# Attention beside a long convolution on one core: the convolution's weights without zeros, two lags per matmul

## The chip, the cores and the metric

The kernel runs on one core of a Trainium2 chip. The core has a matmul engine (TensorE, PE in the profile, with PEld for its weight loads), a vector engine (VectorE, DVE), an engine for activation functions (ScalarE, ACT), a general one (GpSimd, POOL) and SyncE (SP), which here only issues DMAs. The metric is the time of one execution on the device in microseconds (us), less is better.

## The reference

Two independent halves are computed from bf16 inputs of 2048 positions, and their outputs stand side by side in the last dimension (512 + 512 columns).

The first half is softmax attention with 32 heads of 16 channels:

```
qkv = x @ wqkv                          # 2048 x 512 @ 512 x 1536
p   = softmax(q k^T / 4)                # 32 heads, 2048 x 2048 each
a   = (p v) @ wo
```

The second half is a convolution over the whole sequence, one filter of 2048 taps for each of 512 channels:

```
k_shift[t] = sum over m < 4 of k[t-m] * shift_k[:, m]
kv = k_shift * v
y[t] = sum over s <= t of ssm_k[:, t-s] * kv[s]      # written with FFTs in the reference
b  = q * (y + kv * ssm_D)
```

## The kernel before, in words

**Attention.** The scores are made transposed, in blocks of 128 keys x 512 queries for one head. There are 32 x 16 x 4 = 2048 such blocks. `qk_mm` (line 796) makes three or so at once, as a head has only 16 channels (padded to 32 rows) and four row strips of PE can hold four heads. A block fills one of the eight PSUM banks. Banks 0 to 2 and 3 to 5 take turns for ScalarE, bank 6 collects the weighted sums, and bank 7 (`BGB`) serves everything else: projections, the convolution, the output projection, and extra score blocks for VectorE.

`emit_exp` (line 821) has ScalarE take the exponential of two or three banks in one instruction, and writes it to the ring PT. `exp_on_dve` (lines 884 to 905) does it on VectorE for some blocks: one instruction takes a block out of PSUM, five more for two blocks at a time make three terms whose sum is the exponential. `emit_pv` (line 970) multiplies by the values; a block of ScalarE needs one matmul, a block of VectorE three.

In `emit_qk` (lines 734 to 740) a block for VectorE goes to bank 7 if that is free (`dve_block(T, n)`). If it is not, and VectorE has little left to do (`LOW`), the block takes the third of the banks that ScalarE would have used, and ScalarE's instruction covers two banks only.

**The convolution.** A Toeplitz product on PE. `kz_store` reverses the filters, adds `ssm_D` to the tap of lag 0 and stores them to a DRAM scratch tensor. `feed_wr` (line 1152) loads a filter back into a row of the ring WR with a source step of one element per partition, so that partition i holds the filter shifted by i. KV holds the products of key and value; they are the weights of the matmul (`lhsT`), and the filter is what is streamed (`rhs`, 128 columns). In the kernel before, the two halves of the 128 partitions hold neighbouring blocks of 64 positions, interleaved by partition (`KV[ch:128:2]`), and where the other block is missing the weights are zeros. `conv_lags` (line 1187) makes 32 lags for each of 64 steps of 8 channels. Each lag is four matmuls, one per column strip of 32: 64 x 32 x 4 = 8192. `conv_out` copies the result out of bank 7 (line 1207), `conv_turn` turns it round on PE (line 1219) and VectorE multiplies by q (line 1226). KV is filled by a product on VectorE (line 561) into a staging area and spread by four DMAs for each 128 channels (`spread_kv`).

**The order of the work.** The program is straight-line code, with the order made in Python when the kernel is built. A planner keeps a clock per engine, with fixed costs for each kind of instruction, and goes in steps T, one ScalarE instruction of line 821 each. In each step it places the next scores, then the weighted sums of step T - 2, then background work that fits before the next exponential: projection halves and other jobs with due times (`jobs`, `unit_step`), and convolution lags, at most `LAGS` a step, from step `N_OPEN` on and spread by `conv_due` up to step `PLAN`. What is left of PE's time gets filler matmuls on zeros (`warm_up`, line 1382). `release` lets SP issue filter loads at chosen points of PE's order. Semaphores hold each engine to that order; every engine runs its own list strictly in turn.

All DMAs are issued through line 352, on three queues: SP (inputs, filters, KV), POOL (spreading of the queries QT, the convolution's q and output, the attention output) and ScalarE (two first weights and the last store).

Of the kernel before, what the change touches and what calls it, by code (L numbers as in the profile page):

```python
# [13 lines left out]
S = 2048  # L14
# [13 lines left out]
NLAG = S // 64  # L28
PAD = 128
LKZ = PAD + S  # L30
LEFT = 16
LKR = LEFT + S
R_W = 12
R_PT = 16
# [8 lines left out]
LEAD = 2  # L43
YIELD = -4
FIRST = 6
BURST = 2
OVER_C = 0.0
HURRY = 2
LOW = 4.5
# [20 lines left out]
R_PTD = 3  # L70
# [12 lines left out]
PLAN = 588  # L83
# [4 lines left out]
GAP = 5  # L88
# [7 lines left out]
DMA_KB = 394  # L96
X_KB = 200
# [24 lines left out]
WR_KB = 330  # L122
# [132 lines left out]
def bass_concat_heads__mha_block__ssm_conv_h3__prompt_kernel(  # L255
# [13 lines left out]
    kz_ap = nc.dram_tensor("kz_scratch", (C, LKZ), BF16).ap()  # L269
# [10 lines left out]
    def sb(name, shape, dt=BF16):  # L280
# [13 lines left out]
    QN = QNF[:, 0:NB * 256].rearrange("p (t d) -> p t d", t=NB)  # L294
# [13 lines left out]
    PTD = sb("PTD", [128, R_PTD, 3, 2, QB])  # L308
    FR = sb("FR", [128, 2 * QB])
# [7 lines left out]
           for x in (WR[:, R_W - 2, :], WR[:, R_W - 1, :], OUTA[:, :, :].rearrange("p r d -> p (r d)"), VS2[:, :])]  # L317
# [9 lines left out]
    KVF = KV[:, :, :, :, :].rearrange("p o r u g -> p (o r u g)")  # L327
    STG = [KVF[:, 32 * S // 16 * ((c + 1) % 4):32 * S // 16 * ((c + 1) % 4 + 1)].rearrange(
        "p (h o u k g) -> p h o u k g", h=2, o=16, u=NB, k=2) for c in range(4)]
    XN = FR[:, :].rearrange("p (j f) -> p j f", j=2)  # L330
# [66 lines left out]
    d_wr = [DmaSem(sem(f"d_wr{i}")) for i in range(3)]  # L397
# [25 lines left out]
    for c in range(4):  # L423
        src = bass.AP(tensor=v2.tensor, offset=v2[128 * (NB - 1), 128 * c].offset, ap=[[D, 128], [-128 * D, NB], [1, 128]])
        h_vn.append(dma(sp, d_kv[3 + c], VST[c], src, kb=512))
# [18 lines left out]
    h_kv0 = [None, None]  # L444
    h_kv0[0] = pool.op(lambda e: e.memset(KV[:, :, :, :, :].rearrange("p o r u g -> p (o r u g)").bitcast(U32), 0), us=(8.8, 8.9))
# [25 lines left out]
    def ready(u):  # L471
# [8 lines left out]
        return KT_OF[u[1]][0] in h_kt and (u[1] < 3 or h_kv0[1] is not None and at(h_kv0[1]) <= pe.t)  # L480

    def pe_unit(u, bank, parts=(0, 1, 2, 3)):
# [19 lines left out]
        elif kind == "kv":  # L502
# [31 lines left out]
    def evac_unit(u, bank, h):  # L534
# [18 lines left out]
        elif kind == "kv":  # L553
            _, c, i = u
            u0 = NB - 4 - 4 * i
            val = VST[c][:, u0:u0 + 4, :].rearrange("p b (h o g) -> p b h o g", h=2, g=4)
            src = PS[:, bank, :].rearrange("p (b h o g) -> p b h o g", b=4, h=2, g=4)
            for ch in range(2):
                dst = STG[c][:, ch, :, u0:u0 + 4, ch, :].rearrange("p o u g -> p u o g")
                hh = (dve.op if ch else urgent)(  # L560
                    lambda e, dst=dst, ch=ch: e.tensor_tensor(dst, src[:, :, ch], val[:, :, ch], ALU.mult),
                    [h, h_vn[c], h_kv0[c // 3]], us=(0.335, 0.46))
# [3 lines left out]
            if sum(kv_n[0:2]) == 8 and c < 2:  # L566
                load_qn(0, [h])
                open_wr(2, hh, True)
# [13 lines left out]
    def spread_kv(c, hh):  # L582
        for half in range(2):
            for ch in range(2):
                src = STG[c][64 * half:64 * half + 64, ch].rearrange("p o u k g -> p o (u k g)")
                dst = KV[ch:128:2, 16 * c:16 * c + 16, 1 - half, :, :].rearrange("p o u g -> p o (u g)")
                h_kvc[c] = dma(sp, d_kvc[c], dst, src, [hh, h_kvc[c - 1] if c else None] if half + ch == 0 else [], kb=256, rate=210)
# [930 lines left out]
```

## Time and profile before

| | us |
|---|---|
| median of 3 runs | 810.54 (809.68 to 813.88) |
| the profiled execution | 807.64 |
| its span | 805.7 |
| ScalarE busy | 784.9 (97%) |
| PE busy | 745.7 (93%) |
| VectorE busy | 715.1 (89%) |
| POOL busy | 90.4 (11%) |

The granted TensorE clock was 0.999 over the execution. The DMA queues moved 161.44 MB, 150.43 MB of it on SP's queue, which took 58.2% of the time of the 16 DMA engines.

A group's row reads: line, engine, operation, output <- inputs, shapes, count | busy us, mean ns of one | idle time of the engine just before, and what ended it. The mean time of one instruction includes its latency; instructions of one engine overlap at their ends, so counts times means come to more than the busy time. A row with "(+1 forms)" mixes shapes. In a row of waits stand the total, the number and the longest. A row of the timeline begins with its start and its length in us.

### The profile page before, as it was taken

How to read it: one execution, taken by the hardware profiler on the slowest of the kernel's cores; microseconds unless marked ns; L12 is line 12 of the kernel's file. 1: busy time of each engine (PE TensorE's matmuls, PEld its weight loads, DVE VectorE, ACT ScalarE, POOL GpSimd, SP SyncE). 2: the span in 40 equal slices, each digit the busy share in tenths (PEclk: the TensorE clock that was granted, in tenths of full speed). 3: DMA queues.
4: the chain of work that ended last, by engine and by line, in shares of the span. 5: the costliest groups of instructions: out<-in, count | busy, mean ns of one | idle time of the engine just before them, and what ended most of it. 6: DMA issues, size and time to landing. Idle time of an engine off the chain costs nothing.

```text
span 805.7 us, 31982 instructions
## 1 busy us (share of the span) xinstructions
PE 745.7 (93%) x14505; PEld 337.1 (42%) x14505; DVE 715.1 (89%) x1427; ACT 784.9 (97%) x680; POOL 90.4 (11%) x160
## 2 busy tenths in 40 slices
PE   8889998999998989999999989989989899999987
PEld 3333444435444433444433434434443434434444
DVE  5989999999798989898898989889999899889986
ACT  7999999999999999999999999999999999999997
POOL 6200402020100101020010030101003020000000
PEclk9999999999999999999999999999999999999999
DMA  9995277846877671446845657985684663876310
GB/s 244 204 306 175 63 184 227 287 108 215 265 261 240 215 243 59 156 115 235 267 142 206 213 168 254 308 281 193 227 299 138 212 224 129 283 260 216 110 55 28
DMA packets 88101, 161.44 MB, mean 200 GB/s; under 512 B 49216, under 2 KB 53184, under 8 KB 87584
## 3 DMA queue, kind: packets, MB, share of 16 engines
q1 hardware_dynamic: 80976, 150.43, 58.2%
q0 software_dynamic: 5792, 8.66, 3.7%
q8 instruction: 114, 1.87, 0.9%
q10 hardware_dynamic: 1200, 0.33, 0.2%
q14 instruction: 19, 0.16, 0.1%
HBM read 142.87 MB, written 6.42 MB: 185 GB/s over the span
## 4 chain that ended last, share of the span: by engine, by line
ACT 79%; PE 14%; DVE 5%; issue 1%; DMA 1%
ACT PT L821 79%; PE PS L970 5%; PE PS L796 4%; PE PS L1187 1%; DVE PTD L884 1%; DMA QN<-in_B_k_dram 1%; PE PS L512 1%; PE PS L1115 1%; PE PS L630 0%; PE PS L491 0%; DVE PTD L902 0%; DVE DT L1041 0%; DVE PTD L905 0%; DVE FR L892 0%; DVE PTD L896 0%
## 5 line engine op out<-in xcount | busy, mean ns | idle before, releaser
L821 ACT ACTIVATE PT<-PS 128x1024 bf16<-128x1024 f32 (+1 forms) x674 | 781.9, 1362 | 11.5 <-PE PS L796 10.8
L796 PE MATMUL PS<-QT,KTo 32*128 32x512 bf16 (+2 forms) x2248 | 265.6, 364 | 39.8 <-ACT PT L821 17.5
L884 DVE TENSOR_SCALAR PTD<-PS 128x512 uint16<-128x512 f32 x326 | 219.2, 682 | 49.2 <-PE PS L796 47.8
L1187 PE MATMUL PS<-WR,KV 128*26 128x128 bf16 (+9 forms) x8192 | 191.2, 219 | 0.7 <-issue 0.6
L970 PE MATMUL PS<-PT,VA 128*32 128x512 bf16 (+2 forms) x1889 | 184.6, 369 | 5.0 <-DVE DT L1041 2.1
L1187 PEld LDWEIGHTS PS<-WR,KV 128*32 128x32 bf16 (+8 forms) x8192 | 140.6, 94 | 52.9 <-issue 29.8
L796 PEld LDWEIGHTS PS<-QT,KTo 32*128 32x128 bf16 x2248 | 69.6, 91 | 205.0 <-ACT PT L821 150.4
L970 PE MATMUL PS<-PTD,VA 128*32 128x512 bf16 (+1 forms) x1077 | 121.0, 360 | 3.9 <-issue 3.9
L902 DVE TENSOR_TENSOR PTD<-FR,PTD 128x1024 f16<-128x1024 bf16 (+1 forms) x164 | 112.3, 685 | 4.0
L905 DVE TENSOR_TENSOR PTD<-PTD 128x1024 bf16<-128x1024 f16 (+1 forms) x164 | 111.5, 680 | 1.9
L352 POOL DMA_DIRECT2D QT<-QS x120 | 60.4, 511 | 443.7 <-DVE QS L539 443.7
L970 PEld LDWEIGHTS PS<-PT,VA 128*32 128x32 bf16 x1889 | 47.4, 93 | 100.8 <-issue 85.5
L892 DVE TENSOR_SCALAR FR<-PTD 128x1024 uint16<-128x1024 uint16 (+1 forms) x164 | 69.0, 421 | 3.5
L896 DVE TENSOR_SCALAR PTD<-PTD 128x1024 uint16<-128x1024 uint16 (+1 forms) x164 | 68.9, 420 | 0.0
L1382 PE MATMUL PS<-IDN,ZW 128*32 128x512 bf16 (+3 forms) x297 | 67.4, 310 | 1.3 <-issue 1.0
L899 DVE TENSOR_SCALAR PTD<-FR 128x1024 f16<-128x1024 bf16 (+1 forms) x164 | 68.1, 415 | 0.0
L970 PEld LDWEIGHTS PS<-PTD,VA 128*32 128x32 bf16 x1077 | 44.8, 96 | 33.2 <-issue 4.4
L1382 PEld LDWEIGHTS PS<-IDN,ZW 128*32 128x32 bf16 x297 | 23.4, 96 | 23.3 <-issue 12.2
L1041 DVE STREAM_TRANSPOSE DT<-PS 128x512 f32<-128x512 f32 x31 | 22.1, 713 | 5.6 <-PE PS L970 5.3
L352 POOL DMA_DIRECT2D out_dram<-OUTA x15 | 8.6, 575 | 97.2 <-DVE OUTA L1123 93.1
L1115 PE MATMUL PS<-WKV,OTN 128*128 128x512 bf16 (+1 forms) x68 | 19.0, 371 | 0.3 <-DVE OTN L1090 0.3
L523 PE MATMUL PS<-WKV,xT 128*128 128x128 bf16 x256 | 18.3, 220 | 0.4 <-DVE KTo L548 0.3
(75 smaller groups left out, 259.3 us busy)
## 6 DMA issues: line engine op xcount, KB each, us to landing
WR<-kz_scratch SPq DMA_DIRECT2D x256, 512.0 KB, 5.8
KV<-KV SPq DMA_DIRECT2D x16, 256.0 KB, 5.4
kz_scratch<-WR SPq DMA_DIRECT2D x1, 2176.0 KB, 8.8
QN<-in_B_q_dram POOLq DMA_DIRECT2D x2, 1024.0 KB, 7.6
out_dram<-QN POOLq DMA_DIRECT2D x2, 1024.0 KB, 8.3
QT<-QS POOLq DMA_DIRECT2D x120, 16.0 KB, 3.3
out_dram<-OUTA POOLq DMA_DIRECT2D x15, 128.0 KB, 2.0
QN<-in_B_ssm_k_dram SPq DMA_DIRECT2D x1, 1024.0 KB, 8.3
```

The lines of the kernel that those rows point to most:

```text
L352: f(outp, inp).then_inc(dsem.sem, 16)
L796: ins = e.matmul(PS[:, bank, i * w:i * w + w], lhsT=KTo[32 * s:32 * s + 32, OF[n_] % 2, kt * 128:(kt + 1) * 128], rhs=QT[32 * s:32 * s + 3 ...
L821: h_exp[T] = act.op(lambda e: e.activation(PT[:, p0:p0 + n, :].rearrange("p b f -> p (b f)"), PS[:, banks[0]:banks[0] + n, :].rearrange("p ...
L884: st["h"].append(urgent(lambda e: e.tensor_scalar(lin[:, QB * half:QB * half + QB].bitcast(U16), PS[:, bank, :], FIX_ADD, FIX_HI, ALU.add, ...
L892: st["d"] = st["m"] = dve.op(lambda e: e.tensor_scalar(FR[:, w].bitcast(U16), lin[:, w].bitcast(U16), 0x7F, 0x3F80, ALU.bitwise_and, ALU.b ...
L896: dve.op(lambda e: e.tensor_scalar(low[:, w].bitcast(U16), lin[:, w].bitcast(U16), 0xFF80, None, ALU.bitwise_and), [st["h"][-1]], us=us)
L899: st["d"] = dve.op(lambda e: e.tensor_scalar(top[:, w].bitcast(FP16), FR[:, w], T1, T0, ALU.mult, ALU.add), [st["m"]], us=us)
L902: st["d"] = h_last[j] = dve.op(lambda e: e.tensor_tensor(top[:, w].bitcast(FP16), FR[:, w], top[:, w].bitcast(FP16), ALU.mult), [st["d"]], ...
L905: st["d"] = dve.op(lambda e: e.tensor_tensor(top[:, w], top[:, w].bitcast(FP16), lin[:, w], ALU.mult), [st["d"]], us=us)
L970: ins = e.matmul(dst, lhsT=w, rhs=rhs, start=first, stop=last, tile_position=(0, 32 * s))
L1187: ins = e.matmul(PS[32 * g:32 * g + 2 * ((30 - d) // 2 + 1), BGB, c0:c0 + w], lhsT=kv, rhs=WR[:, (4 * qd + g) % R_W, S - 64 * d - 128:S - ...
L1382: pe.op(lambda e, s=s, k=k, rhs=rhs, bank=bank, rows=rows, c0=c0, first=first: e.matmul(PS[32 * s:32 * s + rows, bank, c0:c0 + 128 * k], l ...
```

## The change

The convolution's partitions are laid out anew. Partitions 0 to 63 take positions of the first half of the sequence (0 to 1023) and partitions 64 to 127 those of the second, in blocks of 64. For each lag block the stationary operand holds both halves of the partitions filled with data, and the streamed filter row holds the filter at two offsets that lie 1024 taps apart. One matmul so does what two did, no weights are zeros between, and there are 8 lags for each of 128 steps of 4 channels (`NLAG`, `NQD`): 128 x 8 x 4 = 4096 matmuls, each of 128 streamed columns, with 32, 30, ... 18 columns of weights in place of 32, 32, 30, ... 2.

The filters are stored in DRAM by channel pairs: for each pair and each half of the partitions, 2 x 1088 taps one after the other (`SEG` = 1088). One DMA loads 64 partitions with runs of 2112 elements (4224 bytes), two channels at once; there are 512 such loads in place of 256 of 128 partitions with runs of 4096 bytes. The ring WR has room for 22 of them (11 rows of both halves).

Along with it:

- KV is half as large. Products of key and value go straight to it, in one instruction of 512 columns in place of two of 256, and the second copy for the other half of the partitions is made by one DMA per 128 channels in place of four. The matmuls before it write 64 rows each, two at once. Its second clearing in the middle of the kernel falls away.
- The convolution is done in bursts of four steps (`BURST`) that fill bank 7, and copied out 512 columns at a time; turning the result round takes eight matmuls for 8 steps (16 x 8 = 128) where four transposes for 4 steps (16 x 4 = 64) stood.
- q and the convolution's output are loaded and stored as halves of 64 partitions, four DMAs each in place of two; v is loaded in halves too.
- On VectorE's path for exponentials the three terms get two rings: five buffers for the first term (`PTD`), three for the other two (`RST`), with the steps in another order. `next_blocks` and `dve_block` choose blocks by row strip.
- A block for VectorE is no longer held back from bank 7 when the convolution wants it but has no room in this step (`state["go"]`, `PRESS`).
- Constants of the planner change, R_PT from 16 to 15 among them, and due times of some jobs are spread.

Counted in the lists of the two programs as built (before / after): exponentials of three banks 374 / 463, of two banks 300 / 162; score blocks taken by VectorE 326 / 335; its five-step chains 164 / 169; fillers 297 with 101,504 columns / 564 with 207,360; matmuls in all 14,505 / 11,014.

```diff
-NLAG = S // 64
+NLAG = S // 256
+NQD = C // 4
+SEG = S // 2 + 64
-R_W = 12
-R_PT = 16
+R_W = 22
+R_PT = 15
-BURST = 2
+BURST = 4
-LOW = 4.5
+LOW = 3.0
-PLAN = 588
+PLAN = 600
-WR_KB = 330
+WR_KB = 300
...
-    kz_ap = nc.dram_tensor("kz_scratch", (C, LKZ), BF16).ap()
+    kz_ap = nc.dram_tensor("kz_scratch", (C // 2, 2, 2 * SEG), BF16).ap()
...
-    WR = sb("WR", [128, R_W, S])
+    WR = sb("WR", [128, R_W // 2, SEG + S // 2])
-    KV = sb("KV", [128, C // 8, 2, 2 * NB, 4])
+    KV = sb("KV", [128, NQD, 2 * NB, 4])
...
                 for m in range(4):
-                    c0 = LEFT + 128 * (4 * i + 3 - b) - m
-                    ins = e.matmul(PS[:, bank, 128 * b:128 * b + 128], lhsT=KTR[kt_i][:, kt_c, c0:c0 + 128], rhs=DG[:, c, m, :],
-                                   start=(m == 0), stop=(m == 3))
+                    for x in range(2):
+                        c0 = LEFT + 64 * (4 * i + 3 - b) + S // 2 * x - m
+                        ins = e.matmul(PS[64 * x:64 * x + 64, bank, 128 * b:128 * b + 128], lhsT=KTR[kt_i][:, kt_c, c0:c0 + 64],
+                                       rhs=DG[:, c, m, :], start=(m == 0), stop=(m == 3), tile_position=(0, 64 * x))
...
+            dst = KV[:, 32 * c:32 * c + 32, u0:u0 + 4, :].rearrange("p q w g -> p w q g")
+            hh = urgent(lambda e: e.tensor_tensor(dst, src, val, ALU.mult), [h, h_vn[c]], us=V512)
...
+        src = KV[0:64, 32 * c:32 * c + 32, 0:NB, :].rearrange("p q w g -> p q (w g)")
+        dst = KV[64:128, 32 * c:32 * c + 32, NB:2 * NB, :].rearrange("p q w g -> p q (w g)")
+        h_kvc[c] = dma(sp, d_kvc[c], dst, src, [hh, h_kv0, h_kvc[c - 1] if c else None], kb=256, rate=KV_KB)
...
-        h_kzw[0] = dma(sp, d_kzw, kz_ap.rearrange("(p c) m -> p c m", c=4), KZS, [h, h_kz0], kb=2176)
+        for i in range(4):
+            r, x = i // 2, i % 2
+            dst = kz_ap.rearrange("(p r) x (c m) -> p r x c m", r=2, c=2)[:, r, x, :, :]
+            h_kzw[0] = dma(sp, d_kzw, dst, KZS[:, 2 * r:2 * r + 2, S // 2 * x:S // 2 * x + SEG], [h, h_kz0] if i == 0 else (), kb=557)
...
-        if aside and conv_wants(T):
+        if aside and conv_wants(T) and (state["go"] or conv_due() < T - PRESS):
             return None
...
-        lin, low, top = [PTD[:, j % R_PTD, i, :, :].rearrange("p a n -> p (a n)") for i in range(3)]
+        lin = PTD[:, j % R_PTD, :, :].rearrange("p a n -> p (a n)")
+        low, top = [RST[:, j % R_RST, i, :, :].rearrange("p a n -> p (a n)") for i in range(2)]
...
+            qd, r, x = n // 4, n % 4 // 2, n % 2
+            src = kz_ap[channel(qd) // 2 + r, x, 0:1]
+            src = bass.AP(tensor=kz_ap.tensor, offset=src.offset, ap=[[1, 64], [1, SEG + S // 2]])
+            h_wr[qd] = dma(sp, d_wr[qd % 6], WR[64 * x:64 * x + 64, (2 * qd + r) % (R_W // 2), :], src, [h_kzw[0], dep, h], kb=264, rate=WR_KB, late=2.95)
...
+    def conv_place(qd, g, rows):
+        dst = PS[32 * g:32 * g + rows, BGB, :]
+        c0 = 256 * (1 - qd % 4 // 2) + 64 * (1 - qd % 2)
+        return bass.AP(tensor=dst.tensor, offset=PS[32 * g:32 * g + 1, BGB, c0:c0 + 1].offset, ap=[dst.ap[0], [128, 2], [1, 64]])
...
-                d = DIST[n]
-                w = 64 if d < 0 else 128
                 for g in range(4):
-                    kv = KV[:, qd, (1 + d) % 2, (1 + d) // 2 * 2:2 * NB, g]
-                    ins = e.matmul(PS[32 * g:32 * g + 2 * ((30 - d) // 2 + 1), BGB, c0:c0 + w],
-                                   lhsT=kv, rhs=WR[:, (4 * qd + g) % R_W, S - 64 * d - 128:S - 64 * d - 128 + w],
+                    dst = conv_place(qd, g, 32 - 2 * n)
+                    w0 = SEG * (g % 2) + S // 2 - 128 * n - 128
+                    ins = e.matmul(dst, lhsT=KV[:, channel(qd) // 4, 2 * n:2 * NB, g], rhs=WR[:, (2 * qd + g // 2) % (R_W // 2), w0:w0 + 128],
                                    start=(n == 0), stop=(n == NLAG - 1), tile_position=(0, 32 * g))
...
+        src = bass.AP(tensor=src.tensor, offset=PS[:, BGB, 511:512].offset, ap=[src.ap[0], [-1, 512]])
+        bank_free[BGB] = h_ybw[0] = urgent(lambda e: e.tensor_copy(YB[:, qd % 8 // 4, :], src), [h, h_yb[0]], slack=S_C, us=V512)
...
             for k in range(4):
-                ins = e.transpose(pbf[:, 128 * k:128 * k + 128], YB[:, b % 2, 128 * k:128 * k + 128], IDN[:, :])
+                for part in range(2):
+                    y = YB[:, k // 2, 256 * (k % 2) + 128 * part:256 * (k % 2) + 128 * part + 128]
+                    ins = e.matmul(PS[:, bank, 128 * k + 4 * part:128 * k + 128], lhsT=y, rhs=(own, next_)[part], start=part == 0, stop=part == 1)
```

More of the change, by code (lines that the diff above doesn't have):

```diff
@@ L869, in dve_block @@
             return None
-        rows = [blk(b)[2] for b in bl[:-1]]
-        ahead = [b for b in ahead[:4] if b not in bl]
-        return next((b for b in ahead if blk(b)[2] not in rows), ahead[0] if ahead else None)
+        return pick_row(ahead, 4)
     h_last = {}
@@ L908, in exp_on_dve @@
         dep = lambda: [st["d"]]
-        begin = lambda: (n == 2 or st["alone"]) and (j == 0 or j - 1 in h_last)
+        begin = lambda: (n == 2 or st["alone"]) and (j < R_RST or all((j - R_RST, i) in h_ptd for i in range(len(pairs[j - R_RST]["h"]))))
         if half == 0:
@@ L949, in emit_pv @@
             pv_n[(n, s)] = pv_n.get((n, s), 0) + 1
-            terms = [PTD[:, on_dve[b][0] % R_PTD, i, on_dve[b][1], :] for i in range(3)] if b in on_dve else [PT[:, pt_of[b], :]]
+            terms = [PT[:, pt_of[b], :]] if b not in on_dve else [PTD[:, on_dve[b][0] % R_PTD, on_dve[b][1], :]] + [
+                RST[:, on_dve[b][0] % R_RST, i, on_dve[b][1], :] for i in range(2)]
             hl = 2 * s + n % 2
@@ L991, in conv_done @@
     def conv_done():
-        return state["qd"] == C // 8 and not state["turn"] and not part[0]
+        return state["qd"] == NQD and not state["turn"] and not part[0]
     def pv_step(T):
@@ L1213, in conv_turn @@
     def conv_turn(b, bank):
-        pbf = PS[:, bank, :].bitcast(BF16)
+        own, next_ = [bass.AP(tensor=IDN[:, :].tensor, offset=IDN[0:1, 31:32].offset, ap=[IDN[:, :].ap[0], [-1, n], [32, 4]]) for n in (32, 31)]
         def fn(e):
```

179 lines of the change are left out of this document (88 added, 91 removed).

## The prediction

> **What bounds the kernel now.** I read the shares of the engines first, then the chain that ended last, then the exponentials by shape, then what ScalarE and VectorE wait for.
>
> ```profile
> span 805.7 us, 31982 instructions
> ...
> PE 745.7 (93%) x14505; PEld 337.1 (42%) x14505; DVE 715.1 (89%) x1427; ACT 784.9 (97%) x680; POOL 90.4 (11%) x160
> ...
> ACT 79%; PE 14%; DVE 5%; issue 1%; DMA 1%
> ...
> L821 ACT ACTIVATE PT<-PS 128x1024 bf16<-128x1024 f32 (+1 forms) x674 | 781.9, 1362 | 11.5 <-PE PS L796 10.8
> ```
>
> ScalarE is busy for 97% of the span and carries 79% of the chain, and nearly all its work is one line, the exponential of line 821: 781.9 us, with 10.8 us of waits for the score matmuls of line 796. PE at 93% is a pipelined figure; it matters only where it makes ScalarE wait. So the change is worth what it takes off line 821's total and off those waits, and costs what it adds to them.
>
> The exponentials come in two shapes, by the groups kept apart by form, and at the very end the timeline of ScalarE shows the short one alone and in a row:
>
> ```profile
> L821 ACT ACTIVATE PT<-PS 128x1536 bf16<-128x1536 f32 x374 | 524.9, 1558 | 2.8 <-PE PS L796 2.5
> L821 ACT ACTIVATE PT<-PS 128x1024 bf16<-128x1024 f32 x300 | 301.1, 1117 | 8.7 <-PE PS L796 8.3
> ...
> 796.35 1.02 ACT L821 ACTIVATE PT<-PS 128x1024 bf16<-128x1024 f32 x1 [0.25 <-PE PS L796]
> 797.83 2.88 ACT L821 ACTIVATE PT<-PS 128x1024 bf16<-128x1024 f32 x3 [0.46 <-PE PS L796]
> ```
>
> One short exponential takes 1.02 us alone and three take 2.88, so each further one costs (2.88 - 1.02) / 2 = 0.93 us. The long ones then cost (781.9 - 300 x 0.93) / 374 = 1.345 us. Per block of 512 columns this is 0.465 us in the short form and 0.448 in the long one. The short form also meets most of the waits (8.3 of 10.8 us).
>
> **The change on ScalarE.** Lines 737 to 740 make a short exponential where a block for VectorE has to take one of ScalarE's three banks because bank 7 is occupied, mostly by a convolution. With half the convolution matmuls that bank is free more often. In the instruction list of the changed program, as built, there are 463 long and 162 short exponentials: 1713 blocks in place of 1722, in 625 instructions in place of 674. At the two prices: 463 x 1.345 + 162 x 0.93 = 773.4 us, which is 8.5 us less. One end: if time went by blocks alone, 9 x 0.465 = 4.2 us. The other: the mean times of the two rows, scaled so that they add up to 781.9 (524.9 + 301.1 = 826.0 counts overlaps), are 1.329 and 0.950 us; they give 769.2 us, 12.7 less. I take 8.5, since it rests on intervals and not on latencies.
>
> **The change on PE.** The next rows are the stretch of the convolution, from its first to its last matmul (length, busy time of PE, of its weight loads, VectorE, ScalarE, POOL, then clock, share of the DMA engines, GB/s), a run of convolution matmuls in the timeline, three groups, and three rows of PE's own waits (us in total, times, the longest).
>
> ```profile
> 106.00:767.00 661.00, 617.21 (x12846) 279.78 (x12838) 592.31 (x1169) 652.84 (x565) 59.85 (x112) 1.00 0.63 210
> ...
> 507.45 0.73 PE L1187 MATMUL PS<-WR,KV 128*32 128x128 bf16 x40
> ...
> L1187 PE MATMUL PS<-WR,KV 128*26 128x128 bf16 (+9 forms) x8192 | 191.2, 219 | 0.7 <-issue 0.6
> L523 PE MATMUL PS<-WKV,xT 128*128 128x128 bf16 x256 | 18.3, 220 | 0.4 <-DVE KTo L548 0.3
> L1382 PE MATMUL PS<-IDN,ZW 128*32 128x512 bf16 (+3 forms) x297 | 67.4, 310 | 1.3 <-issue 1.0
> ...
> PE PS L970 <- issue: 5.2, 7, 1.3
> PE PS L796 <- DVE PTD L884: 2.7, 8, 0.6
> PE PS L970 <- DVE DT L1041: 2.1, 6, 0.5
> ```
>
> The run is ten groups of four matmuls (four column strips), the first ten of a step, with 32 to 24 columns of weights; it takes 0.73 us, of which one matmul's own 0.22 is the drain: (0.73 - 0.22) / 9 = 0.057 us per group. The new form has 8 lags x 128 steps = 1024 groups in place of 2048, of the same 128 columns, so PE gets back 1024 x 0.057 = 58 us, or at 0.73 / 10 = 0.073 each, 75 us, at most. Against it: turning the result round becomes 128 matmuls in place of 64, at 18.3 / 256 = 0.071 us each 4.6 us; the key-value product has 512 in place of 256, which costs 0 if two column halves run side by side, as four strips do above, or 256 x 0.071 = 18 us if not. I take 0, because the strips are the nearer row. The fillers of line 1382 rise from 297 (101,504 columns) to 564 (207,360), by 67.4 x 207,360 / 101,504 - 67.4 = 70 us of busy time, but they are put only where PE would wait. So PE's share will hardly fall, and the 58 us shorten nothing by themselves. What they can shorten is the 10.8 us: the share of the waits that stands behind convolution bursts and short exponentials. Ends: all 10.8 gone, or 5 us more, if PE's own waits for issue and for VectorE (5.2 + 2.7 + 2.1 = 10 us in the rows above) grow by half and all of it reaches ScalarE. I take 3 us, a bit over a quarter, as the short form, which has 8.3 of them, falls by nearly half while code fetches and projections keep theirs.
>
> [...]
>
> **The change on VectorE.**
>
> ```profile
> L884 DVE TENSOR_SCALAR PTD<-PS 128x512 uint16<-128x512 f32 x326 | 219.2, 682 | 49.2 <-PE PS L796 47.8
> L902 DVE TENSOR_TENSOR PTD<-FR,PTD 128x1024 f16<-128x1024 bf16 (+1 forms) x164 | 112.3, 685 | 4.0
> L905 DVE TENSOR_TENSOR PTD<-PTD 128x1024 bf16<-128x1024 f16 (+1 forms) x164 | 111.5, 680 | 1.9
> L892 DVE TENSOR_SCALAR FR<-PTD 128x1024 uint16<-128x1024 uint16 (+1 forms) x164 | 69.0, 421 | 3.5
> L896 DVE TENSOR_SCALAR PTD<-PTD 128x1024 uint16<-128x1024 uint16 (+1 forms) x164 | 68.9, 420 | 0.0
> L899 DVE TENSOR_SCALAR PTD<-FR 128x1024 f16<-128x1024 bf16 (+1 forms) x164 | 68.1, 415 | 0.0
> ...
> L1207 DVE CAST YB<-PS 128x256 bf16<-128x256 f32 x32 | 13.3, 416 | 5.8 <-PE PS L1187 3.0 <-PE PS L970 2.3 <-PE PS L1382 0.4
> L1123 DVE CAST OUTA<-PS 128x512 bf16<-128x512 f32 x15 | 10.2, 682 | 0.4 <-PE PS L1115 0.4
> ```
>
> Nine more blocks: 9 x 219.2 / 326 = 6.1 us. Five more runs of the five-step chain (169 in place of 164): 5 x (112.3 + 111.5 + 69.0 + 68.9 + 68.1) / 164 = 13.1 us. The copy out of the convolution's bank is 512 wide in place of 256: 32 x (0.682 - 0.416) = 8.5 us. The 32 half products of key and value become 16 whole ones, about even. The sum is 28 us: 743 us busy of 794, 94%. VectorE's idle time falls from 91 to 51 us; 47.8 of the 91 were waits for score matmuls, which hide the additions, so on the path I count nothing. If that cover is gone, the rows above in which PE waits for VectorE (2.7 and 2.1 us) grow first.
>
> **The change on the queues.**
>
> ```profile
> WR<-kz_scratch SPq DMA_DIRECT2D x256, 512.0 KB, 5.8
> ...
> L352 SPq DMA_DIRECT2D WR<-kz_scratch x256: 512/606/1702, 50.5 to 751.0; - x128
> ...
> q1 hardware_dynamic: 2129, 7.74, 55.0%
> ...
> q1 hardware_dynamic: 4160, 1.05, 79.0%
> ...
> q1 hardware_dynamic: 5070, 1.34, 109.7%
> ```
>
> The filter loads become 512 of 64 partitions x 4224 bytes in place of 256 of 128 x 4096: 138.4 MB for 134.2. SP issues 256 more at 0.606 us, 155 us more on a queue that mostly waits. The last three rows are 40 us with filter loads alone on the queue (400 to 440 us), 6.5 us of a copy KV to KV whose source is 64 partitions (350 to 356.5), and 6 us of loads of v into all 128 partitions (22 to 28). The filter loads run at 7.74 / (0.55 x 40) = 352 GB/s of engine time. The copy and the loads of v, both in runs of 256 bytes, make 1.05 / (0.79 x 6.5) = 204 and 1.34 / (1.097 x 6) = 204. So no row shows large runs into half the partitions. Bounds of one new load: 270,336 bytes at 352 GB/s, 0.77 us, and at 204, 1.33 us. I take 0.85, near the first, because run length is nearest to it and the half source made no difference between the two slow rows. Then 512 x 0.85 = 435 us, plus about 29 us of other traffic (210 GB/s x 661 us = 138.8 MB less 129 MB of filters, at 333 GB/s), fit into 661 us and the loads stay hidden. The four stores of the filters in place of one add three issues of 0.5 us on SP ahead of the first filter loads; the first convolution is at 106 us, tens of us later. Four more halves of v are the same bytes. KV to KV falls from 16 issues to 4. POOL issues four more DMAs for q and the convolution's output, at SP's 0.606 us some 2.4 us on an engine at 11%, and clears half as much of KV. All these I cost at nothing; what hides them is that slack before 106 us and POOL's idle time.
>
> **The sum.** 805.7 - 8.5 - 3.0 = 794.2 us of span. The profiled execution took 807.64 us, 1.94 over its span: 796.1. The median shown, 810.54, is 0.36% above it, so I predict 799 us. From the ends of the terms, in the same way: savings of 4.2 and 0 give 806 us, savings of 12.7 and 10.8 give 787, and 5 us lost in place of the 3 gained 807.
>
> **The rivals.**
>
> *Late filters (slower).* If each load takes the upper 1.33 us, 512 of them need 681 us, with the other traffic 710 us, in a stretch of 661. PE stands in order, so a convolution that waits for WR holds the scores behind it, and ScalarE stops: at least 49 us more, 799 + 49 = 848 us. The ring holds 22 half rows and a burst uses 16, so the queue cannot run on far ahead, and more is likely. It decides from (661 - 29) / 512 = 1.23 us per load. For it: a load uses half the partitions, and the mean demand of 210 GB/s is above the 204 of those rows. Against: equal rates of half and whole at short runs. [...] 16%.
>
> *VectorE gives it back (no change).* If, at 94%, its blocks come late by what the 8.5 us had gained, PE waits with the weighted sums queued behind them: about 808 us. For it is the 91 us of idle that becomes 51; against, that most of the 91 was waiting for PE. 10%.
>
> *Dearer convolution (slower).* Nothing shows matmuls that write two runs of 64 columns 512 bytes apart. If a group costs twice 0.057 us, PE gets nothing back while its order leaves room for half: 58 us late in bursts; a third of it on ScalarE gives 799 + 20 = 819 us. Against: 64-column forms stand among today's at the same pace. 6%.
>
> **Numbers.** Faster 68%, with its own range of 787 to 806; no change 10%; slower 22% (both others). Half a per cent, about 4 us, is what runs of this kernel can tell apart. For 8 in 10 the range takes the forecast, no change and the nearer slower case: 787 to 822; late filters lie above it.
>
> **What would show it.** Right: line 821 at about 773 us in 625 instructions, its waits at 8 us or less, the convolution's line at 4096 matmuls, filter loads below 1 us apart, VectorE near 743 us. Wrong: waits of the convolution's line for DMAs, DMA share near 1.0 through the middle, waits of line 821 for the scores of several tens of us, or waits of PE for VectorE above 15 us.

## The result and the profile after

The changed kernel takes 845.39 us (median of 4 runs, 841.35 to 849.87), the kernel before 811.08 us (median of 4, 809.68 to 813.88). The ratio is 1.042, with an interval of 1.036 to 1.048: the change makes the kernel slower, by 34 us. The profiled execution took 849.87 us, with a span of 848.1, against 807.64 and 805.7 before.

From the page of the kernel after: span, busy times, granted clock and DMA share in 40 slices, SP's queue, the chain that ended last, and two groups.

```profile
span 848.1 us, 25239 instructions
...
PE 751.9 (89%) x11014; PEld 306.7 (36%) x11014; DVE 731.5 (86%) x1445; ACT 783.3 (92%) x631; POOL 90.3 (11%) x163
...
PEclk9999999988999999979799998999979999999999
DMA  9995276989597779699994879999998997998100
...
q1 hardware_dynamic: 77696, 151.49, 75.2%
...
ACT 52%; PE 27%; DVE 16%; issue 4%; DMA 1%
...
L825 ACT ACTIVATE PT<-PS 128x1536 bf16<-128x1536 f32 (+1 forms) x625 | 780.4, 1394 | 55.8 <-PE PS L800 54.9
...
L1205 PE MATMUL PS<-WR,KV 128*26 128x128 bf16 (+7 forms) x4096 | 93.0, 224 | 18.7 <-issue 17.5
```

The two profiled executions lie 42.4 us of span apart, the medians 34. ScalarE has nearly the same work as before (783.3 us busy, 784.9 before). Its waits for the scores went from 10.8 to 54.9 us: those 44.1 us are the loss between the two profiles. ScalarE's part of the chain fell from 79 to 52%, PE's and VectorE's rose. The DMA engines moved about the same bytes (151.49 MB, 150.43 before) but were occupied 75.2% of the time in place of 58.2%, and in many slices over 90%. The granted clock (the share of its full speed that PE was given), 0.999 before, has dips: between 100 and 800 us it stands at 0.5 for 55 us in all, where the kernel before has no such stretch. Its mean is 0.967.

What PE waited for in the kernel after (us in total, times, the longest; beside these stand 19.2 us in which the scores wait for ScalarE, 17.5 before):

```profile
PE PS L1205 <- issue: 17.5, 9, 3.2
PE PS L800 <- DVE PTD L892: 15.5, 41, 1.0
PE PS L979 <- issue: 7.0, 5, 2.4
...
PE PS L1205 <- DMA WR<-kz_scratch: 1.1, 1, 1.1
```

Almost none of it is a wait for filters (1.1 us). 24.5 us are waits "for issue": PE stands still and this view names nothing that holds it (what does is worked out further down). Before, this was 5.2 us in the weighted sums and 0.6 in the convolution. Waits of the scores for VectorE rose from 2.7 to 15.5 us.

One such halt in the timeline of PE, kernel after (start, length, matmuls, idle time before):

```profile
408.04 0.39 PE L800 MATMUL PS<-QT,KTo 32*128 32x512 bf16 x3
408.37 0.39 PE L979 MATMUL PS<-PT,VA 128*32 128x512 bf16 x1
411.19 0.61 PE L979 MATMUL PS<-PT,VA 128*32 128x512 bf16 x3 [2.43 <-issue]
411.21 1.45 PE L1205 MATMUL PS<-WR,KV 128*32 128x128 bf16 x32
...
413.78 1.87 PE L1234 MATMUL PS<-IDN,YB 128*128 128x128 bf16 x8
415.59 0.61 PE L800 MATMUL PS<-QT,KTo 32*128 32x512 bf16 x3
...
421.66 0.39 PE L800 MATMUL PS<-QT,KTo 32*128 32x512 bf16 x3
```

After 2.43 us of halt the same three score matmuls take 0.61 us instead of 0.39, until about 421: PE runs slower for nearly 10 us after it stood for 2.4. Around it, by time (columns as in the prediction; the last three are the granted clock, the DMA share and GB/s), first the slow stretch with its granted clock of 0.50, and at the end SP's queue from 400 to 440 us:

```profile
410.70:421.00 10.30, 9.81 (x88) 3.66 (x91) 5.19 (x10) 5.55 (x4) 0.00 (x0) 0.50 1.03 254
...
360.00:400.00 40.00, 34.27 (x501) 13.58 (x500) 30.31 (x59) 33.43 (x28) 3.99 (x8) 0.87 0.96 226
400.00:440.00 40.00, 35.95 (x519) 14.71 (x519) 31.82 (x64) 33.96 (x28) 0.00 (x0) 0.87 0.98 239
...
q1 hardware_dynamic: 2799, 9.46, 96.9%
```

The DMA engines are full. SP's queue moves 9.46 / (0.969 x 40) = 244 GB/s of engine time, where the same 40 us before gave 352. A filter load of 270,336 bytes so takes 1.11 us, not 0.85. (The expectations below say 253 GB/s and 1.07 us; these rows give 244 and 1.11.)

### The profile page after: what moved, and what is told of

It reads as the page before. It is cut to its first block, busy times and chain, and to the rows that moved or that the text cites. A ratio compares the mean times of both kernels' runs of the same rounds, so it can differ in the third digit from the quotient of the medians.

```text
span 848.1 us, 25239 instructions
## 1 busy us (share of the span) xinstructions
PE 751.9 (89%) x11014; PEld 306.7 (36%) x11014; DVE 731.5 (86%) x1445; ACT 783.3 (92%) x631; POOL 90.3 (11%) x163
## 3 DMA queue, kind: packets, MB, share of 16 engines
q1 hardware_dynamic: 77696, 151.49, 75.2%
## 4 chain that ended last, share of the span: by engine, by line
ACT 52%; PE 27%; DVE 16%; issue 4%; DMA 1%
ACT PT L825 52%; PE PS L979 9%; PE PS L800 7%; DVE PTD L892 5%; PE PS L1234 3%; PE PS L1205 2%; DVE RST L907 2%; DVE RST L913 2%; PE PS L1403 2%; DVE RST L904 1%; DVE RST L900 1%; DMA WR<-kz_scratch 1%; DVE RST L910 1%; PE PS L1124 1%; DVE QN L1241 1%
## 5 line engine op out<-in xcount | busy, mean ns | idle before, releaser
L825 ACT ACTIVATE PT<-PS 128x1536 bf16<-128x1536 f32 (+1 forms) x625 | 780.4, 1394 | 55.8 <-PE PS L800 54.9
L800 PE MATMUL PS<-QT,KTo 32*128 32x512 bf16 (+2 forms) x2248 | 252.4, 372 | 52.7 <-ACT PT L825 19.2
L1403 PE MATMUL PS<-IDN,ZW 128*32 128x512 bf16 (+3 forms) x564 | 130.8, 328 | 1.3 <-issue 0.9
L907 DVE TENSOR_TENSOR RST<-RST 128x1024 f16<-128x1024 bf16 (+1 forms) x169 | 114.8, 681 | 2.7
L913 DVE TENSOR_TENSOR RST<-RST,PTD 128x1024 bf16<-128x1024 f16 (+1 forms) x169 | 114.3, 676 | 0.0
L1205 PE MATMUL PS<-WR,KV 128*26 128x128 bf16 (+7 forms) x4096 | 93.0, 224 | 18.7 <-issue 17.5
L979 PE MATMUL PS<-RST,VA 128*32 128x512 bf16 (+1 forms) x736 | 95.8, 369 | 1.8 <-issue 1.8
L900 DVE TENSOR_SCALAR RST<-PTD 128x1024 uint16<-128x1024 uint16 (+1 forms) x169 | 70.8, 420 | 20.3 <-PE PS L979 19.4
L1205 PEld LDWEIGHTS PS<-WR,KV 128*26 128x26 bf16 (+7 forms) x4096 | 71.0, 103 | 45.3 <-issue 33.7
L904 DVE TENSOR_SCALAR RST<-RST 128x1024 f16<-128x1024 bf16 (+1 forms) x169 | 70.5, 418 | 2.4
L910 DVE TENSOR_SCALAR RST<-PTD 128x1024 uint16<-128x1024 uint16 (+1 forms) x169 | 69.9, 413 | 1.3
L979 PE MATMUL PS<-PTD,VA 128*32 128x512 bf16 (+1 forms) x368 | 68.8, 371 | 1.4 <-issue 1.4
```

The source lines that it names most:

```text
L800: ins = e.matmul(PS[:, bank, i * w:i * w + w], lhsT=KTo[32 * s:32 * s + 32, OF[n_] % 2, kt * 128:(kt + 1) * 128], rhs=QT[32 * s:32 * s + 3 ...
L825: h_exp[T] = act.op(lambda e: e.activation(PT[:, p0:p0 + n, :].rearrange("p b f -> p (b f)"), PS[:, banks[0]:banks[0] + n, :].rearrange("p ...
L900: st["d"] = dve.op(lambda e: e.tensor_scalar(low[:, w].bitcast(U16), lin[:, w].bitcast(U16), 0x7F, 0x3F80, ALU.bitwise_and, ALU.bitwise_or ...
L904: st["d"] = dve.op(lambda e: e.tensor_scalar(top[:, w].bitcast(FP16), low[:, w], T1, T0, ALU.mult, ALU.add), [st["d"]], us=us)
L907: st["d"] = dve.op(lambda e: e.tensor_tensor(top[:, w].bitcast(FP16), low[:, w], top[:, w].bitcast(FP16), ALU.mult), [st["d"]], us=us)
L910: dve.op(lambda e: e.tensor_scalar(low[:, w].bitcast(U16), lin[:, w].bitcast(U16), 0xFF80, None, ALU.bitwise_and), [st["d"]], us=us)
```

## The experiments

Three questions: do the filter loads cause the loss, and if so their number, their size or the partitions that they go to? What else lies beside them? And does the forecast hold with both taken away? Where a ratio is given, it is to the kernel before on the same chip, with its interval. The runs were made on two chips, on which the kernel before had medians of 814 to 816 us, against 811.08 in the result above; so kernels that did not run side by side are better compared by their ratios than by their times.

**The kernel after with little filter traffic.** All loads after the first 22 move 64 elements per partition instead of 2112; their number, order and waits stay.

```diff
-            src = bass.AP(tensor=kz_ap.tensor, offset=src.offset, ap=[[1, 64], [1, SEG + S // 2]])
+            src = bass.AP(tensor=kz_ap.tensor, offset=src.offset, ap=[[1, 64], [1, SEG + S // 2 if n < R_W else 64]])
```

> The changed kernel with every filter load after the first 22 cut to 64 partitions x 128 bytes (in place of 4224); the order of all engines is the same. From the second use of a ring row on the filters are stale, so the convolution's values are not computed. Theory A (filter loads of half the partitions move at 253 GB/s, 1.07 us each, keep the queues full, and PE's code fetches stand behind them; PE halts 2 to 3 us and its clock falls): waits of line 825 fall from 54.9 to 10 to 25 us, the clock returns to 0.99 or more, time 803 to 818 us. Theory B (the turning matmuls of line 1234, 29.9 us busy in place of some 9, hold the scores back): still over 830 us. Theory C (VectorE's new ring and order come late): still over 830 us, with 15 us of waits of PE for line 892.

Measured: 812.81 us, ratio 0.9979 (0.9955 to 1.0004). The page's row of ScalarE's exponentials, the group of VectorE's product with q, and PE's first waits:

```profile
L825 ACT ACTIVATE PT<-PS 128x1536 bf16<-128x1536 f32 (+1 forms) x625 | 777.6, 1400 | 19.9 <-PE PS L800 18.7
...
L1241 DVE TENSOR_TENSOR QN<-PS,QN 128x512 bf16<-128x512 f32 x16 | 11.1, 692 | 18.8 <-PE PS L1234 18.8
...
PE PS L800 <- ACT PT L825: 19.6, 51, 1.0
PE PS L800 <- DVE PTD L892: 15.2, 41, 1.0
```

33 us of the 34 are gone, by the ratios (1.042 and 0.9979) all of them. The waits for issue are gone too (the longest sum on one line is 1.0 us), and ScalarE's waits are 18.7 us in place of 54.9. So the bytes of the filter loads are what costs, not their 512 issues, which are still there. The run does not price the halves alone: it also lacks what whole loads would cost, as the kernel before pays it. What stays are 15.2 us in which scores wait for VectorE, and 18.8 us in 16 pieces in which VectorE waits for the turn (line 1234). The next run looks at that.

**The turn with a permuted copy of the identity.** The kernel after reads the identity for the turn backwards and in steps of 32 elements. Here VectorE writes it once, in that order, to a tile of its own, and the turn reads contiguous columns.

```diff
+    h_idp = dve.op(lambda e: e.tensor_copy(IDP[:, :].rearrange("p (b g) -> p b g", g=4), bass.AP(
+        tensor=IDN[:, :].tensor, offset=IDN[0:1, 31:32].offset, ap=[IDN[:, :].ap[0], [-1, 32], [32, 4]])), [h_idn], us=(0.15, 0.28))
...
-        own, next_ = [bass.AP(tensor=IDN[:, :].tensor, offset=IDN[0:1, 31:32].offset, ap=[IDN[:, :].ap[0], [-1, n], [32, 4]]) for n in (32, 31)]
+        own, next_ = IDP[:, :], IDP[:, 0:124]
```

> The changed kernel with the permuted identity of the turning matmuls copied once into a tile of its own, so that they read 128 and 124 neighbouring columns in place of steps of 32 and -1. Same result, same planned order. Both theories: line 1234 falls from 29.9 us busy to 10 to 12, and the multiplication by q no longer waits 19 us for it. Theory A: 3 to 15 us off 845. Theory B: 25 us or more off, 820 us or less.

Measured: 839.48 us, ratio 1.0314 (1.0255 to 1.0373), 6 us less than the kernel after, or 1.1% by the ratios. Their intervals just overlap, so the gain can be 2 us or 15. ScalarE's waits are 38.5 us, PE's waits for issue 15.3 + 5.1 + 1.7: with the filter traffic in place the halts stay. Whether they hide a part of what the turn costs is not shown.

**Both together.** Little traffic and the permuted copy.

> The changed kernel with both edits: filter loads after the first 22 cut to 128 bytes a partition (later filters stale), and the turning matmuls reading a contiguous permuted identity. If the two causes are all there is, it reaches the forecast of 795 to 802 us: 13 us less than the run with little traffic alone. Waits of line 825 fall from 18.7 to 12 us or less, and PE's waits for VectorE's line 892 from 15 to 8 us or less, because VectorE no longer stands before the multiplication by q. If VectorE's new ring is a third cause, PE still waits 10 us or more for line 892 and the time stays at 803 to 810 us.

Measured: 798.53 us (798.38 to 798.60), ratio 0.9804 (0.9756 to 0.9852). The page's busy times and exponentials, then PE's waits for VectorE and ScalarE's waits for scores; lines of this kernel are 3 higher:

```profile
span 796.9 us, 25204 instructions
...
PE 711.2 (89%) x10978; PEld 297.0 (37%) x11014; DVE 735.4 (92%) x1446; ACT 776.6 (97%) x631; POOL 91.0 (11%) x163
...
L828 ACT ACTIVATE PT<-PS 128x1536 bf16<-128x1536 f32 (+1 forms) x625 | 773.6, 1457 | 7.0 <-PE PS L803 6.5
...
PE PS L803 <- DVE PTD L895: 10.1, 30, 0.9
...
ACT PT L828 <- PE PS L803: 6.5, 16, 1.0
```

The turn is worth 14 us here (812.81 to 798.53, and as much by the ratios). PE's waits for VectorE fell to 10.1 us, not to the 8 or less expected. The first turn in the timeline, with little traffic and the strided reading, and then with the copy:

```profile
144.53 1.87 PE L1234 MATMUL PS<-IDN,YB 128*128 128x128 bf16 x8 [0.48 <-DVE YB L1221]
```

```profile
149.46 0.61 PE L1237 MATMUL PS<-IDP,YB 128*128 128x128 bf16 x8 [0.48 <-DVE YB L1224]
```

Eight matmuls take 1.87 us with the strided identity and 0.61 with the copy. 16 turns: 16 x (1.87 - 0.61) = 20 us of PE, as PE's busy time says too (730.8 to 711.2 us). PE and VectorE stand in order, so each turn held back the scores behind it on PE and 1.2 us of VectorE.

**Halves or number?** In the kernel before, each filter load is cut in two: in one kernel by partitions (0 to 63, then 64 to 127, still 4096 bytes each), in the other by columns (all 128 partitions, 2048 bytes each). Number, bytes and plan are the same in both.

```diff
-            src = bass.AP(tensor=kz_ap.tensor, offset=kz_ap[row, 0].offset, ap=[[1, 64], [64 * LKZ, 2], [1, S]])
-            h_wr[qd] = dma(sp, d_wr[qd % 3], WR[:, n % R_W, :], src, [h_kzw[0], dep, h], kb=512, rate=WR_KB, late=2.95)
+            for x in range(2):
+                src = bass.AP(tensor=kz_ap.tensor, offset=kz_ap[row, 32 * x].offset, ap=[[1, 32], [64 * LKZ, 2], [1, S]])
+                h_wr[qd] = dma(sp, d_wr[qd % 3], WR[64 * x:64 * x + 64, n % R_W, :], src, [h_kzw[0], dep, h], kb=256, rate=WR_KB, late=2.95)
```

> The kernel before, with each filter load of 128 partitions x 4096 bytes cut into two of 64 partitions x 4096 bytes. Nothing else is changed but what the planner makes of the halves. Theory A: packets of these loads get slower, the DMA share of the convolution's stretch rises from 0.63 to 0.85 or more at the same bytes, PE's waits for issue rise, and the time goes from 811 to 820 to 850 us. Theories B and C: 811 us within 1%.

```diff
+            for x in range(2):
+                src = bass.AP(tensor=kz_ap.tensor, offset=kz_ap[row, S // 2 * x].offset, ap=[[1, 64], [64 * LKZ, 2], [1, S // 2]])
+                h_wr[qd] = dma(sp, d_wr[qd % 3], WR[:, n % R_W, S // 2 * x:S // 2 * x + S // 2], src, [h_kzw[0], dep, h], kb=256, rate=WR_KB, late=2.95)
```

> The kernel before, with each filter load cut into two of 128 partitions x 2048 bytes: as many DMAs of as many bytes as in the run with half the partitions, in the same planned order. Theory A, as half the partitions: DMA share 0.63 to 0.70, 808 to 818 us. If it is the number of DMAs or their size and not the partitions, it loses as much as the run with halves.

Measured: halves 894.98 us, ratio 1.0989 (1.0967 to 1.1011); short runs into all partitions 816.09 us, ratio 1.0033 (1.0007 to 1.0059). SP's queue and the first waits of PE and of ScalarE, halves first, then short runs:

```profile
q1 hardware_dynamic: 85072, 150.45, 72.4%
...
PE PS L970 <- issue: 23.8, 10, 4.1
PE PS L796 <- ACT PT L821: 19.7, 50, 1.0
PE PS L1188 <- issue: 19.0, 11, 4.2
PE PS L796 <- issue: 13.2, 7, 3.4
...
ACT PT L821 <- PE PS L796: 92.6, 85, 5.2
```

```profile
q1 hardware_dynamic: 117840, 150.45, 60.0%
...
PE PS L970 <- issue: 7.6, 9, 1.2
PE PS L796 <- issue: 5.1, 3, 2.1
...
ACT PT L821 <- PE PS L796: 18.7, 34, 2.0
```

Loading halves alone, with nothing else changed, brings a fuller queue (72.4% of the longer span, where the kernel before had 58.2), the halts and 80 us, more than the 820 to 850 us expected. Twice as many loads of half the run length bring 0.3%, some 3 us. It is the halves.

**Which 64 partitions?** In the kernel before, the loads after the first 12 are cut to 64 partitions, once to 0 to 63 and once to 32 to 95; the other half keeps old filters. Bytes and number are equal.

```diff
+            p0, p1 = (0, 128) if n < R_W else (0, 64)      # the other kernel: (32, 96)
...
+            src = bass.AP(tensor=kz_ap.tensor, offset=kz_ap[row, p0 // 2].offset, ap=[[1, (p1 - p0) // 2], [64 * LKZ, 2], [1, S]])
```

> The kernel before, each filter load after the first 12 cut to partitions 0 to 63 (64 x 4096 bytes; the other half of the row stays stale, so half of the filter rows is not renewed). Half the bytes, one DMA each. If it matters which partitions of the 128 a load writes, as the next run tests: 253 GB/s of engine time, a DMA share of filter loads of about (67 MB / 253 GB/s) / 805 us = 33%.

> The same with partitions 32 to 95. [...] If any 64 partitions are slow, for instance because an engine has only four rows a load, both shares are equal.

Measured, one run each: 801.55 and 801.81 us, where the kernel before had a median of 816.06 on that chip, and 811.35 as the lowest of 14 runs. The stretch of the convolution and the loads' median time to landing, partitions 0 to 63 first, then 32 to 95:

```profile
106.00:767.00 661.00, 616.33 (x12880) 280.28 (x12894) 597.94 (x1181) 657.62 (x570) 61.05 (x113) 1.00 0.48 114
...
WR<-kz_scratch SPq DMA_DIRECT2D x244, 256.0 KB, 4.3
```

```profile
106.00:767.00 661.00, 616.54 (x12884) 280.42 (x12904) 598.67 (x1182) 657.95 (x571) 60.97 (x113) 1.00 0.37 114
...
WR<-kz_scratch SPq DMA_DIRECT2D x244, 256.0 KB, 3.4
```

The same 114 GB/s occupy the DMA engines 48% of the time in one case and 37% in the other. So 64 partitions are not slow as such: 0 to 63 are, 32 to 95 are not. In the trace a packet of these loads takes 305 ns in the median in the first kernel and 159 in the second. With half the bytes neither costs time, since the queue has room. The runs show something else: the kernel before is itself faster with half of its filter bytes.

**The new layout with whole loads.** The two sets of 64 positions are interleaved by partition again, so that one load fills all 128 partitions with a pair of channels; the products go through a staging tile from which three DMAs spread them, and the ring has 20 half rows. One kernel keeps loads of 64 partitions with this layout, one has 256 whole loads (and `WR_KB` 330), one adds the permuted copy.

```diff
-            src = kz_ap[channel(qd) // 2 + r, x, 0:1]
-            src = bass.AP(tensor=kz_ap.tensor, offset=src.offset, ap=[[1, 64], [1, SEG + S // 2]])
-            h_wr[qd] = dma(sp, d_wr[qd % 6], WR[64 * x:64 * x + 64, (2 * qd + r) % (R_W // 2), :], src, [h_kzw[0], dep, h], kb=264, rate=WR_KB, late=2.95)
+            src = kz_ap[channel(qd) // 2 + r, 0, 0:1]
+            src = bass.AP(tensor=kz_ap.tensor, offset=src.offset, ap=[[1, 64], [2 * SEG, 2], [1, SEG + S // 2]])
+            h_wr[qd] = dma(sp, d_wr[qd % 6], WR[:, (2 * qd + r) % (R_W // 2), :], src, [h_kzw[0], dep, h], kb=528, rate=WR_KB, late=2.95)
```

> The changed kernel with the partitions interleaved as in the kernel before (two positions' halves side by side: the product of key and value goes to a staging tile and is spread over the partitions by three DMAs for each 128 channels), and a ring WR of 10 rows in place of 11 to make room. Filter loads still of 64 partitions, 0 to 63 or 64 to 127, 512 of them. It is the control for the next run. Theory A: as slow as the changed kernel, 840 to 865 us, packets of 4224 bytes at about 280 ns. If the layout by halves of the sequence were what costs: 810 us.

> The same interleaved layout and ring, but a filter load writes all 128 partitions (64 positions x 2 halves, runs of 4224 bytes): 256 loads of the same bytes; planner's price 330 in place of 300. Theory A: DMA share of the middle falls from 0.9 to 0.65, PE's waits for issue from 25 to 8 us, time 808 to 816 us, as the run with little traffic. If it is the bytes and not the half partitions: 835 us or more.

> The run with whole-partition loads, with the contiguous permuted identity as well: two lags per matmul with neither of the two costs. If both causes are additive: 797 to 806 us, faster than the kernel before by 0.7 to 1.8%. If VectorE or something else holds the rest: 806 to 812 us, no change.

Measured: 852.44 us with half loads, ratio 1.0478 (1.0413 to 1.0542); 824.35 with whole loads, 1.0113 (1.0078 to 1.0148), more than the 808 to 816 us expected; 808.67 with whole loads and the copy, 0.9936 (0.9907 to 0.9964), more than the 797 to 806 us expected if the two costs were all. Whole loads win back 28 us and the copy 16 more. The planner's rate is a second difference between the first two; changed the other way in the last run below, it moved the kernel after by 1 us, or 0.7% by the ratios. Of the last kernel, the page's span, busy times, SP's queue and exponentials, one wait of VectorE and the longest of PE for issue:

```profile
span 805.0 us, 24926 instructions
...
PE 713.4 (89%) x10975; PEld 296.8 (37%) x11010; DVE 730.3 (91%) x1431; ACT 778.9 (97%) x634; POOL 91.2 (11%) x163
...
q1 hardware_dynamic: 90112, 153.58, 57.3%
...
L830 ACT ACTIVATE PT<-PS 128x1536 bf16<-128x1536 f32 (+1 forms) x628 | 776.0, 1439 | 12.7 <-PE PS L805 12.2
...
DVE SG L567 <- DMA KV<-SG: 7.8, 1, 7.8
...
PE PS L1210 <- issue: 1.2, 1, 1.2
```

This version beats both kernels, by 0.6% over the one before. The queue is back at 57%, the halts are 1.2 us. VectorE waits once, for 7.8 us at about 110 us, until the staging tile is free.

**Taking that wait away.** A product is now planned only 9 us after the planned landing of the DMA before it.

```diff
-        return KT_OF[u[1]][0] in h_kt
+        return KT_OF[u[1]][0] in h_kt and (u[1] < 2 or h_kvc[u[1] - 1] is not None and at(h_kvc[u[1] - 1]) + 9.0 <= pe.t)
```

> The run with whole-partition loads and the contiguous permuted identity, with one wait of its own taken away: there VectorE stood 7.8 us at 110 us for the copy out of the staging tile; here the product for the next 128 channels is not due until 9 us after the planner's landing of that copy. Expected 798 to 803 us, 1 to 2% under the kernel before; if the 7.8 us were hidden, 808 us again.

Measured: 811.42 us, ratio 0.9934 (0.9903 to 0.9966). The wait is gone, and no time is gained: ScalarE's waits are 17.6 us (12.2 with the wait), one halt for issue of 2.8 us among their causes. That expectation missed; the 7.8 us were not on the path, or others took their place.

**A planner that knows the price.** The kernel after, with `WR_KB` 265 in place of 300: the planner counts 1.0 us per load and spreads the loads accordingly.

```diff
-WR_KB = 300
+WR_KB = 265
```

> The changed kernel with the planner's price for a filter load raised from 264/300 = 0.88 to 264/265 = 1.00 us (measured: 1.07). Loads as before, of half the partitions. If the harm comes only from a plan that does not know the rate, code fetches get their gaps back and the time falls to 815 to 830 us. If the queues are simply too full for PE's code, it stays above 835 us.

Measured: 844.1 us, ratio 1.0347 (1.0313 to 1.0382), against 845.39 and 1.042 for the kernel after. The waits for issue are fewer (6.2 + 3.9 + 3.0 us) but ScalarE's are still 46.5 us. The queue is as full as in the kernel after, 75.2%, and by the ratio 28 us of loss remain: at most a small part of it is one of the plan.

## Why the prediction was wrong

I forecast 799 us with a range to 822; it is 845.39. The step that failed is that 512 loads of 0.85 us fit into the stretch "and the loads stay hidden", at no cost: they take 1.11 us each, fill the DMA engines, and PE and with it ScalarE stand still. That is worth 28 us between half and whole loads of one layout (852.44 and 824.35). The turn is the second, smaller failure.

*The price of a filter load.* I bounded it by 0.77 and 1.33 us and took 0.85, "because run length is nearest to it and the half source made no difference between the two slow rows". It is 1.11 us. The flaw is in the second reason: both slow rows have runs of 256 bytes, where half and whole came to 204 GB/s alike; at some 4 KB they are 244 and 352, so the equality of the short rows said nothing about long ones. Nor is it the mere number of partitions: in the kernel before, loads of 0 to 63 took a DMA share of 0.48 where loads of 32 to 95 took 0.37 for the same bytes. Why these differ no run shows.

*The point from which it decides.* I let late filters decide from 1.23 us per load, the mean that fits the stretch. At 1.11 us, the mean still fits, as the DMA share of the stretch shows, and PE waits only 1.1 us for filters:

```profile
106.00:767.00 661.00, 586.17 (x8611) 232.98 (x8608) 576.89 (x1128) 608.29 (x489) 60.28 (x111) 0.96 0.88 209
```

The price is paid elsewhere and earlier: at a share of 0.96 to 0.98 over tens of us, PE halts "for issue" up to 3.2 us at a time. Shown is that these halts come with the halved loads (56 us on three lines in the kernel before with halves, 12.7 on two with short runs) and go with their bytes. By the times in the trace, what ends them are packets of the instruction queue, which I take for PE's own code. The rows of that queue, in the kernel after and before:

```profile
q8 instruction: 87, 1.43, 0.8%
...
q8 instruction: 114, 1.87, 0.9%
```

Its packets have 16,384 bytes, and in both kernels one starts for each 256 records of PE (matmuls, weight loads, semaphore instructions; 87 packets for 22,378 records, 114 for 29,355), a block that the planner counts too (`BLOCK`). After the first 100 us the kernel after has 14 halts for issue of over 0.4 us. All of them lie at the border of two blocks (193 or 194 records past a multiple of 256), and each ends 1.3 to 1.6 us after the end of such a packet; no border is passed sooner than that. The 26 such halts in the kernel before with halves also end 1.3 to 1.7 us after a packet. The packets are late more than they are long: from 106 to 767 us they start 3.2 us in the median after PE passed the border before, against 2.1 us in the kernel before, and over the whole span they take 1258 ns, against 966. This rests on the times in the traces; no run changes these packets alone.

So the rival of late filters had the cause, with the wrong place for the wait and too high a threshold; at 16% it had too little weight. That its 848 us lie so near is luck: they come from 1.33 us per load and from waits for filters, and neither is what was measured. Of my own signs for a wrong forecast, three came: the DMA share near 1.0, tens of us of waits of line 825, and waits for VectorE above 15 us. The fourth, the convolution waiting for DMAs, did not.

*The turn.* I costed its matmuls at 0.071 us each, from a row with contiguous columns: 4.6 us for the 64 that are added. All 128 took 16 x 1.87 = 30 us, since they read the identity in steps of 32 and backwards (the two were undone together), 20 us more than with contiguous columns; undoing that gained 14 to 16 us where the queue had room, and 6 us, of uncertain size, where it had not. The diff showed the stride, and I had not weighed it: eight of these matmuls take 1.87 us with it (run with little traffic) and 0.61 with the copy (both together). Why it costs more no run shows.

*What held.* With both taken away, ScalarE's line is 773.6 us (773.4 forecast), its waits 6.5 (7.8), the whole 798.53 (799). VectorE was 731.5 us busy and 735.4 there (743), and its cover held, though the scores wait for it 10.1 us in place of 2.7. The convolution's matmuls are no dearer with two runs of 64 columns (224 ns in the mean, 219 before), and halving their number brought PE from 745.7 to 711.2 us of busy time although fillers doubled; the rivals of VectorE and of a dearer convolution are out as causes of the 34 us. One reservation: that run has no filter traffic to speak of, and the kernel before gains too when half of its own is cut (801.55 against 816.06, one run). So 798.53 fits the sum on the engines, and does not show that the change could give 1.4% with its transfers. That it meets 799 within 1 us is in part luck: to the kernel before on its chip it is 0.9804, where the forecast was 799 / 810.54 = 0.986. The best with real transfers is 808.67. Where the 10 us between the two lie stays open; the one candidate tried, the wait for the staging tile, is not it.

## What to carry to other kernels

Before costing a DMA, write down which partitions it touches, not only how many and how long the runs are: halves at 0 and 64 cost 1.11 us where a whole load's rate gives 0.77, and the rows with packets of 256 bytes (204 GB/s for half and whole) said nothing on it. A transfer can be hidden on average and still cost: a DMA share of 0.96 to 0.98 over tens of us, as here, was a bound of its own, seen as 24.5 us of "issue" waits of PE and a granted clock of 0.967 in the mean rather than as waits for the data (1.1 us). And price every new access pattern of a matmul by a row with the same stride.

## What the runs showed of the hardware

- In both kernels one packet of 16,384 bytes of the instruction queue came for each 256 records of PE (114 for 29,355 before, 87 for 22,378 after), and PE passed no border of these blocks sooner than 1.2 us after its packet (1.3 in the kernel after, both from 100 us on). The 14 waits for "issue" of over 0.4 us in the kernel after (from 100 us on) ended 1.3 to 1.6 us after such a packet.
- After a halt of 2.43 us, PE ran slower for nearly 10 us (0.61 us for three scores instead of 0.39, granted clock 0.50). Not each halt does that: after one of 2.78 us, up to 749.9 us, the granted clock stayed at 1.00.
- A matmul of the turn, of 128 or 124 columns, whose moving operand is read in steps of 32 elements and backwards follows the one before after (1.87 - 0.39) / 7 = 0.21 us; contiguous, after (0.61 - 0.22) / 7 = 0.056 us (0.39 and 0.22 us are one matmul's own time). The strided eight took the same 1.87 us at a granted clock of 1.00 (at 144.53 us with little traffic) and of 0.50 (at 413.78 us in the kernel after).
- In the kernel before, a packet of 4096 bytes took 159 ns in the median in loads of all 128 partitions, the same 159 in loads of 32 to 95, and 305 in loads of 0 to 63.
- Doubling the number of loads at half the run length (2048 bytes) raised the share of SP's queue only from 58.2 to 60.0%.
